# Early denominators in a tile of their own, low words converted on GpSimd, and a new order table, in an attention and feed-forward kernel with a built-in planner

## The chip, the core and the metric

The kernel runs on one core of one Trainium2 chip. The metric is the device time of one execution in microseconds; lower is better. Below, PE is the matrix engine, DVE the vector engine, ACT the scalar engine, POOL the GpSimd engine, and SP the queue from which this kernel issues all its DMAs.

## The reference

Linear attention with exponential features over 8 batches, 8 heads, 576 tokens and head size 64, then a feed-forward layer over 4608 tokens:

```python
def phi(x):
    proj = einsum('bhsd,df->bhsf', x, w_phi)                 # d = 64, f = 128
    proj = proj - max(abs(proj), axis=-1, keepdims=True)
    return concatenate([exp(proj), exp(-proj)], axis=-1)
q_p, k_p = phi(q), phi(k)
kv  = einsum('bhsf,bhsd->bhfd', k_p, v)
z   = sum(k_p, axis=2)
num = einsum('bhsf,bhfd->bhsd', q_p, kv)
den = einsum('bhsf,bhf->bhs', q_p, z)[..., None] + 1e-06
x   = (num / den) as [4608 tokens, 512]
h   = x @ w_in                                               # 512 x 2048
out = maximum(h, 0) ** 2 @ w_out                             # 2048 x 512
```

The two weight matrices arrive as 64-bit words, each of a high and a low 32-bit half.

## The kernel before

**Pairs.** Attention is done for 32 pairs of heads, p = 0 to 31; four pairs make a batch. The first six pairs are done by `early(p)`, the others by `visit` and `late`. For an early pair the steps are: project the keys (L604, L610), take the greatest absolute value of each row and subtract it on DVE (L620, L623, L630, L633), exponentials on ACT (L626 to L638), key-value product on PE (L660, L665, L693), eviction and transposition (`kvs`, `kz`, L705); the same for the queries (L721, L727, L732, L734, L755, L764, L766); numerators (L774, evicted into `n`), denominators (L791). The denominators of pair p are copied from PSUM by `copy` (L310) into the scratch tile `sx`, from there a DMA (L799) takes four rows of `sx` into `den`, DVE adds and inverts (L808, L809), a DMA writes `rd` (L812) and two more spread it into `rb` (L819). DVE multiplies `rb` by `n` (L826); ACT and DVE split the product into two 16-bit parts and write them into the token ring (L845, L848).

**Scratch.** `sx` has one buffer and two kinds of user: the early denominators, and `batch_scale`, whose ACT scans (L567) write their elementwise result there only to have somewhere to write it; what counts is their accumulator, the greatest absolute value of each pair's `v`. `batch_scale` of the first batch needs the scans of v_0 to v_3; its result goes through a DVE reduction (L572, tile `m`), a transposition on PE (L397) and a few short DVE operations.

**Weights.** There are 16 pieces of 1024 KB, 8 of `w_in` (raw0i to raw7i) and 8 of `w_out` (raw0o to raw7o). `join_words` turns the word pairs of a piece into one float, tile `u`. It scales the high half (`size`, ACT L451), converts the low half to three bits (`low`: ACT L460, DVE or POOL L462, by the piece's number in `order_w`), and joins them. Pieces of even number write the low half as 16-bit values into the lower half of the high word (`low_half`) and need `shift` (L465) and `join` (L472); those of odd number write 32-bit values (`low_word`) and need `ends` (L468) and `join_shift` (L476). `w_in` then needs its greatest value (`most`, ACT L498), a scale (`power`, PE L397, DVE L403 to L408) and two parts (`value_in`, ACT L547, DVE L550); `w_out` three parts (L517; L306 on POOL or DVE; L535 on ACT or L537 on DVE).

**Feed-forward.** Tokens go in 18 chunks of 256, the hidden dimension in 8 steps: the first product (L1027, 24 matmuls into `ph`), three ACT operations (L1036, L1038, L1040), one on DVE (`gl`, L306), and the second product (L1057, 12 matmuls into `po`). The first chunk needs the ring entries of pairs 0 to 3, and step f needs piece f of both matrices.

**The order.** Every operation is given to a planner (`Plan`) with an engine, a time in us, what it follows and which tiles it uses; some have a second engine (`other`). `order` simulates the engines with these times and takes at each step the ready operation of the lowest rank; the instructions are then written engine by engine in that order, and each engine works through its list in order. The ranks of the early operations come from the table `RANKS`, two characters for each. Tiles with one buffer and several kinds of user (`single`) are free again at `open_at`. Where `lock` is given, the planner lets DVE and POOL operations delay each other.

Of the kernel before, what the change touches and what calls it, by code (L numbers as in the profile page):

```python
# [292 lines left out]
def tile_kernel(ctx, tc, qp, kp, vp, w_phi, w_in, w_out, out):  # L293
# [269 lines left out]
    def batch_scale(b, rank):  # L563
        last = []
        for i in range(NP):
            p = b * NP + i
            last.append(P.add("ACT", 0.78, lambda p=p, i=i: A.activation(  # L567
# [103 lines left out]
    def early(p):  # L671
# [127 lines left out]
        o = P.add("SP", 0.65, lambda: SP.dma_start(  # L799
            den_[p], sx_["d", p][0:128:32, 0:SH].rearrange("j (r x) -> j r x", x=9)), [o], use + [("den", p)],  # L800
# [354 lines left out]
    "IfI<I3=WN$W(Y>a6S2MOP)TpPYLwQJ@TBuI#N%NGIFF;HZLSMHA5>EICS3O?LrRGJJF_@$G]Q-P,JELKGI=OD(P3GXUyO`NnR{K`"
    "NuV#MsLmL0WO[lV-N>E>=IT8Q^WIE*O$MZIYDuO.H5Lx?:I(FiMdE0K=LVM*T5M<J+HoAsHZQ?LeS_M>S>LjI9WCQjAQEa:(:o<J"
    "=ZC!=$;HC)?+Co7(6(?l?B5N<k@>?=@u9@9l73?-F.BMBm>?JwH^LMLY@JMh>*+y:L3qF[?UCX<`5K?hG_]0B-AyB7@ZC^EXE[CV"
    "N_DXRHKlI6QL@J@QDNPrFxNoO0NjHeL(N_RWZ0FEE9KTH,G$R;D(H4>EC<5h:JBhE_CiHUIGJIC%FT:2B!=RDKP?8XA|F)BTMl;Z"
    "?RHe:89c@wA<>*;<=L?oAX<?7dAo3J>[D21M?<7I46;T<&:/B!FWK_KKJ_O0LdEu>*1s;TE,BJGeOfR8U}PnJtVuLIYgB/FuG0B."
    "Dq7wF#@V?2==319hGfM.JLLzPMY17zB[A[A.@4@ZF7HaVQRBMaK7R}Cu?<HxB4FaBX@Q6rCk;IC+D-:*/DKcJHGpOGE*T0QaDOPO"  # L1160
    "RNEC_U^gP]AOETIxATILM6G5=rQ^C0<tB<OaJeTjT7LMY*L>L{IiK?Ht@S>.R*QYO]PZLkIn:4Jd9wBY>dSeJSWlN>G}CsPRKp<z"
    ";]>nIK^SD-F^6oAhGfR1MSVKD.4W?0AqB|8t77HOAj@OL-CY@{A-KXB8PfN[Q{L0NBM(KqHBMxKi?r<V7n19<+BFDFMyC(P|XFZ/"
    "LXI)L%:&D%Ke?XT{M8U>BvR9LeE.E=</?D;u>=B25D=_9e0i:K,u5g4@0T&o1h#22G9`8I:,7x8+Av>Z0*20*{$&(V.[9Z>5J_UJ"
# [47 lines left out]
```

## Time and profile before

| | |
|---|---|
| median of 3 runs | 1077.39 us (1074.45 to 1078.67) |
| span of the profiled execution, first to last instruction | 1074.6 us |
| mean granted clock of PE | 0.984 |
| PE busy | 1032.4 us, 96% of the span |
| DVE busy | 742.0 us, 69% |
| ACT busy | 632.7 us, 59% |
| POOL busy | 140.5 us, 13% |
| first matmul of the first product (L1027) | 112.46 us |

For the profiled execution the page gives the span alone. It is 2.8 us under the median of the runs and lies at the lower end of what they spread over. Shares are averages over the whole span; a table of stretches of time is needed to see where an engine waits.

### The profile page before, as it was taken

How to read it: one execution, taken by the hardware profiler on the slowest of the kernel's cores; microseconds unless marked ns; L12 is line 12 of the kernel's file. 1: busy time of each engine (PE TensorE's matmuls, PEld its weight loads, DVE VectorE, ACT ScalarE, POOL GpSimd, SP SyncE). 2: the span in 40 equal slices, each digit the busy share in tenths (PEclk: the TensorE clock that was granted, in tenths of full speed). 3: DMA queues.
4: the chain of work that ended last, by engine and by line, in shares of the span. 5: the costliest groups of instructions: out<-in, count | busy, mean ns of one | idle time of the engine just before them, and what ended most of it. 6: DMA issues, size and time to landing. Idle time of an engine off the chain costs nothing.

```text
span 1074.6 us, 19448 instructions
## 1 busy us (share of the span) xinstructions
PE 1032.4 (96%) x7675; PEld 708.0 (66%) x7762; DVE 742.0 (69%) x1550; ACT 632.7 (59%) x1125; POOL 140.5 (13%) x70
## 2 busy tenths in 40 slices
...
GB/s 361 185 131 114 131 127 44 67 76 56 65 61 80 58 50 72 56 76 57 76 46 74 53 58 45 64 56 76 43 53 28 48 11 42 12 21 20 1 21 20
DMA packets 66143, 73.47 MB, mean 68 GB/s; under 512 B 35204, under 2 KB 44036, under 8 KB 64004
## 3 DMA queue, kind: packets, MB, share of 16 engines
q1 hardware_dynamic: 66052, 72.22, 21.3%
q8 instruction: 61, 1.00, 0.4%
...
## 4 chain that ended last, share of the span: by engine, by line
PE 83%; DVE 1%; issue 1%; ACT 0%
PE po L1057 34%; PE ph L1027 33%; PE pv L660 4%; PE pn L878 3%; PE pp L604 2%; PE pv L878 2%; PE pp L948 2%; PE pn L948 1%; PE pv L665 1%; PE pn L610 1%; DVE wl L537 0%; DVE gl L306 0%; PE pn L397 0%; DVE den L808 0%; ACT sx L567 0%
## 5 line engine op out<-in xcount | busy, mean ns | idle before, releaser
L1027 PE MATMUL ph<-ring,win 128*128 128x256 f16 x3456 | 399.7, 273 | 0.2 <-DVE gl L306 0.2
L1027 PEld LDWEIGHTS <-win 128*128 128x128 f16 x3456 | 336.2, 98 | 69.8 <-issue 8.7
L1036 ACT ACTIVATE r<-ph,cw 128x512 f32<-128x512 f32 x144 | 98.9, 687 | 241.0 <-PE ph L1027 240.7
L306 DVE TENSOR_TENSOR gl<-ph,gh 128x512 bf16<-128x512 f32 x144 | 98.3, 682 | 174.7 <-ACT ph L1040 171.6
L961 POOL PARTITION_ALL_REDUCE mx<-pt x52 | 113.2, 2176 | 618.6 <-ACT pt L310 363.0
L1057 PE MATMUL po<-wh,gh 128*128 128x512 f32 x576 | 171.6, 419 | 0.0
L1057 PE MATMUL po<-wl,gl 128*128 128x512 bf16 x560 | 147.1, 379 | 0.9
L1057 PE MATMUL po<-wl,gh 128*128 128x512 bf16 x505 | 134.6, 381 | 4.7
L1057 PEld LDWEIGHTS po<-wh,gh 128*128 128x128 f32 x576 | 98.5, 189 | 29.2 <-issue 10.9
L1057 PEld LDWEIGHTS <-gl 128*128 128x128 bf16 x576 | 56.4, 98 | 68.0
L1038 ACT ACTIVATE gh<-r 128x512 fp32r<-128x512 f32 x144 | 90.6, 629 | 4.8 <-PE po L1057 0.5
L1057 PEld LDWEIGHTS <-gh 128*128 128x128 bf16 x576 | 44.8, 98 | 73.3 <-issue 39.7
L1040 ACT ACTIVATE ph<-r 128x512 f32<-128x512 f32 x144 | 84.1, 584 | 0.3
L660 PE MATMUL pv<-e,v 128*64 128x256 f32 x512 | 62.6, 385 | 0.8 <-ACT n L310 0.6
L975 DVE SCALAR_TENSOR_TENSOR pt<-qe,zc,pt 128x576 f32<-128x576 f32 x52 | 42.3, 815 | 26.0 <-ACT pt L973 25.4
L310 ACT ACTIVATE n<-pn 128x320 f32<-128x320 f32 (+1 forms) x32 | 13.7, 429 | 70.9 <-PE pn L878 69.3
L626 ACT ACTIVATE e<-e 128x512 f32<-128x512 f32 x64 | 39.7, 621 | 23.8 <-DVE e L623 23.7
L306 DVE TENSOR_TENSOR qe<-pt,mx 128x576 f32<-128x576 f32 x52 | 39.1, 752 | 16.7 <-POOL mx L961 16.3
L660 PEld LDWEIGHTS pv<-e,v 128*64 128x64 f32 x512 | 36.2, 139 | 17.3 <-issue 1.8
L966 ACT ACTIVATE qe<-qe 128x576 f32<-128x576 f32 x52 | 35.0, 672 | 19.8 <-DVE qe L306 19.8
L912 DVE STREAM_TRANSPOSE kvs<-pv 128x256 f32<-128x256 f32 x26 | 11.6, 447 | 48.6 <-PE pv L878 46.0
L973 ACT ACTIVATE pt<-qe,zc 128x576 f32<-128x576 f32 x52 | 40.1, 773 | 4.2
...
## 6 DMA issues: line engine op xcount, KB each, us to landing
v<-in_vp_dram SPq DMA_DIRECT2D x32, 320.0 KB
k<-in_kp_dram SPq DMA_DIRECT2D x32, 288.0 KB
q<-in_qp_dram SPq DMA_DIRECT2D x32, 288.0 KB
...
raw0i<-in_w_in_dram SPq DMA_DIRECT2D x1, 1024.0 KB
```

What stands on the lines that cost most here:

```text
L306: eng.tensor_tensor(out=out_, in0=a, in1=b_, op=ALU.subtract)
L626: o = P.add("ACT", act_us(512), lambda n=n: A.activation(out=e_[n][:, :, 1, :], in_=e_[n][:, :, 0, :], func=AF.Exp, scale=-1.0), [o], [("e ...
L660: PE.matmul(out=to[64 * h:64 * h + 64, 0:256], lhsT=v_[p][:, t, h, :], rhs=e_[2 * p + h][:, t].rearrange("p s f -> p (s f)"), start=t == 0 ...
L878: PE.matmul(out=to[64 * h:64 * h + 64, :], lhsT=kz_[n][:, 128 * s_ + 64 * h:128 * s_ + 64 * h + 64], rhs=qe_[2 * n + h].rearrange("p (s x) ...
L961: o = P.add("POOL", par_us(S), lambda n=n, h=h: G.partition_all_reduce(mx_[n], pt_[p][:, h, :], channels=128, reduce_op=bass_isa.ReduceOp. ...
L973: o = P.add("ACT", act_us(S, 1), lambda h=h, qe=qe, y=y: A.activation(out=y(), in_=qe(0), func=AF.Copy, scale=zc_[p][:, 2 * h:2 * h + 1]), ...
L975: o = P.add("DVE", dve_us(S), lambda h=h, qe=qe, y=y: V.scalar_tensor_tensor(out=y(), in0=qe(1), scalar=zc_[p][:, 2 * h + 1:2 * h + 2], in ...
L1027: PE.matmul(out=ph[:, j, :], lhsT=win[w][:, t, 128 * ff:128 * ff + 128], rhs=ring[half][x][:, t, c0:c0 + T], start=k == 0, stop=k == 3 * K ...
L1036: o = P.add("ACT", act_us(512, 1), lambda: A.activation(out=r_[n], in_=ph_[bank], func=AF.Relu, scale=cw[:, f, 0:1]), [g1], [("ph", bank), ...
L1038: sq = P.add("ACT", act_us(512), lambda: A.activation(out=gh_[n], in_=r_[n], func=AF.Square), [o], [("r", n), ("gh", n)], Q)
L1040: o = P.add("ACT", 0.59, lambda: A.activation(out=ph_[bank], in_=r_[n], func=AF.Square), [o], [("ph", bank), ("r", n)], Q, other=("DVE", 0 ...
L1057: PE.matmul(out=po_[po[i][1]], lhsT=g[:, j, 128 * i:128 * i + 128], rhs=w[:, j, :], start=(ff == 0 and s == 0), stop=(ff == 2 * NFP - 1 an ...
```

## The change

The early denominators are evicted into a tile `dn` of their own (one buffer, 128 x 288) in place of `sx`, and the DMA into `den` reads that tile. All 16 low halves are converted on POOL as 16-bit values, and all pieces use `shift` and `join`; L460, L468 and L476 are no longer issued. In the planner a single tile counts as free when the DMA that reads it has landed (`op.there`), not when it is issued (`op.end`), and four costs are altered. The table `RANKS` is another one throughout.

```diff
-                open_at[tag] = max(open_at.get(tag, 0.0), op.end + self.HOP[op.eng])
+                open_at[tag] = max(open_at.get(tag, 0.0), op.there + self.HOP[op.eng])
...
+    dn_ = tiles(at, "dn", [128, SH], F32, 1)
...
         def low(E):
-            to = (low_half if n % 2 == 0 else low_word)()
+            to = low_half()
...
-        x = (("ACT", 1.15, A, None), ("DVE", 0.68, V, 4.0), ("DVE", 0.68, V, 4.0), ("POOL", 2.4, G, 0.0))[n % 4]
-        l = P.add(x[0], x[1], lambda: low(x[2]), [sz], [], rank, lock=x[3])
-        if n % 2 == 0:
+        l = P.add("POOL", 1.15, lambda: low(G), [sz], [], rank, lock=0.0)
+        if True:
             o = P.add("DVE", 0.68, shift, [sz], key, rank, lock=4.0)
             o = home_read[home] = P.add("DVE", 1.22, join, [o, l], key, rank, lock=4.0)
...
-        most_in[f] = ... P.add("ACT", 1.06, most, [o], [("u", n)], rank)
+        most_in[f] = ... P.add("ACT", 1.2, most, [o], [("u", n)], rank)
...
-                P.add("DVE", 0.69, lambda: near(V), at, key, rank, lock=0.6, other=("ACT", 1.06, lambda: near(A), None))]
+                P.add("DVE", 0.69, lambda: near(V), at, key, rank, lock=4.0, other=("ACT", 1.06, lambda: near(A), None))]
...
-            last.append(P.add("ACT", 0.78, lambda p=p, i=i: A.activation(     # the scans of v
+            last.append(P.add("ACT", 0.82, lambda p=p, i=i: A.activation(
...
-        use = [("sx", ("d", p))]
+        use = [("dn", p)]
...
-        first, second = copy(SH, lambda: sx_["d", p][:, 0:SH], lambda: pn_["d", p][:, 0:SH])
+        first, second = copy(SH, lambda: dn_[p], lambda: pn_["d", p][:, 0:SH])
...
-            den_[p], sx_["d", p][0:128:32, 0:SH].rearrange("j (r x) -> j r x", x=9)), [o], use + [("den", p)],
+            den_[p], dn_[p][0:128:32, :].rearrange("j (r x) -> j r x", x=9)), [o], use + [("den", p)],
...
-            o = P.add("DVE", dve_us(S), lambda h=h, qe=qe, y=y: V.scalar_tensor_tensor(
+            o = P.add("DVE", 0.82, lambda h=h, qe=qe, y=y: V.scalar_tensor_tensor(
...
-    ">e8[J.LRL]EQRBCsO#Ij?@IlF+FbHa@4DoEsJ%^S^INpLYIVR=PXNlY^ADJUQ^J`CNEmD{HgLQLSIeL(UZL[L(F^KXLxC#DLBV<5"
+    "<qBAE1E)s^H&zzcLa5V*AUf&DrX2o]yH.gH[I?MG/a0+M+CD1*hmN<O+4TsLOCZpL)JrM7KOm#c1VeP|9MRTO^W4L9I9SKv@a$F*"
```

What the table moves is read from the order in which the instructions stand. The number at a row's start is its place on its engine; numbers after a name are those of the buffer. Lines below L351 carry a number one higher after the change (L465 becomes L466), up to where both agree again in `split_in`.

The first place is ACT around the scans of v (L567, which write `sx` and the accumulator `vm`). Before, the scan of v_3 stands behind the eviction of denominators 0 into the same scratch:

```order
26 L451 ACTIVATE u_1_341<-raw1i_142 128x1024
27 L567 ACTIVATE sx_2_352,vm_0_157<-v_2_144 128x640
28 L310 ACTIVATE sx_3_363<-pn_4_343 128x288
29 L764 ACTIVATE qe_2_371<-pp_2_356 128x2x288
30 L766 ACTIVATE qe_2_371<-pp_2_356 128x2x288
31 L567 ACTIVATE sx_4_400,vm_0_157<-v_3_163 128x640
32 L498 ACTIVATE raw1i_142,wm_0_93<-u_1_341 128x1024
```

The same engine after the change:

```order
15 L567 ACTIVATE sx_2_263,vm_0_143<-v_2_126 128x640
16 L567 ACTIVATE sx_3_266,vm_0_143<-v_3_138 128x640
17 L310 ACTIVATE kvs_0_281<-pv_0_218 128x384
18 L567 ACTIVATE sx_4_284,vm_1_285<-v_4_140 128x640
19 L498 ACTIVATE raw0i_124,wm_0_93<-u_0_216 128x1024
20 L626 ACTIVATE e_3_287<-e_3_287 128x4x128
21 L628 ACTIVATE e_3_287<-e_3_287 128x4x128
22 L452 ACTIVATE u_1_319<-raw1i_147 128x1024
```

The four scans of the first batch now stand in rows 2, 3, 15 and 16, ahead of the second weight piece; denominators 0 go to `dn_0` in row 36 and denominators 1 to the same buffer in row 52. On SP, the loads of v_2 and v_3 stood in rows 13 and 15 behind five weight pieces, and stand in rows 9 and 10 behind one.

The second place is POOL at the start (L306 is the low part of `w_out`, L462 or L463 the conversion of low halves). Before:

```order
8 masks.py:199 AFFINE_SELECT ident_72<-ident_72 128x128
9 L462 TENSOR_SCALAR raw2i_140<-raw2i_140 128x1024
10 L306 TENSOR_TENSOR wl0_691<-u_4_581,wh0_676 128x1024
11 L306 TENSOR_TENSOR wl0_691<-u_2_513,wh0_676 128x1024
12 L306 TENSOR_TENSOR wl1_938<-u_6_869,wh1_921 128x1024
13 L462 TENSOR_SCALAR raw4i_126<-raw4i_126 128x1024
14 L306 TENSOR_TENSOR wl1_938<-u_8_1003,wh1_921 128x1024
```

After:

```order
11 L463 TENSOR_SCALAR raw0o_308<-raw0o_308 128x1024
12 L463 TENSOR_SCALAR raw2i_185<-raw2i_185 128x1024
13 L463 TENSOR_SCALAR raw1o_166<-raw1o_166 128x1024
14 L463 TENSOR_SCALAR raw3i_145<-raw3i_145 128x1024
15 L306 TENSOR_TENSOR wl0_642<-u_2_523,wh0_621 128x1024
16 L826 TENSOR_TENSOR rb_0_598<-n_0_384,rb_0_598 128x576
17 L463 TENSOR_SCALAR raw2o_719<-raw2o_719 128x1024
18 L306 TENSOR_TENSOR wl0_642<-u_4_560,wh0_621 128x1024
19 L463 TENSOR_SCALAR raw4i_170<-raw4i_170 128x1024
20 L463 TENSOR_SCALAR raw3o_154<-raw3o_154 128x1024
21 L463 TENSOR_SCALAR raw5i_180<-raw5i_180 128x1024
```

Rows 9 and 10 there are the conversions of raw0i and raw1i. POOL does ten conversions, two low parts and one product with `rb` up to row 21; before it did two conversions and four low parts up to row 14.

The third place is DVE at the ring entry of pair 3 (the last L848 row), the last one that the first chunk needs. Before:

```order
126 L468 SCALAR_TENSOR_TENSOR raw4i_126<-raw4i_126 128x1024
127 L476 SCALAR_TENSOR_TENSOR u_7_999<-u_7_999,raw4i_126 128x1024
128 L472 SCALAR_TENSOR_TENSOR u_8_1003<-raw3o_184,u_8_1003 128x1024
129 L732 TENSOR_REDUCE qm_5_1056<-pp_11_1031 128x4
130 L462 TENSOR_SCALAR raw5i_177<-raw5i_177 128x1024
131 L734 TENSOR_TENSOR pt_5_1062<-pp_11_1031,qm_5_1056 128x512
132 L732 TENSOR_REDUCE qm_5_1056<-pp_11_1031 128x4
133 L537 CAST wl1_938<-u_8_1003 128x1024
134 L734 TENSOR_TENSOR pt_5_1062<-pp_11_1031,qm_5_1056 128x512
135 L826 TENSOR_TENSOR rb_3_1052<-n_3_956,rb_3_1052 128x576
136 L468 SCALAR_TENSOR_TENSOR raw5i_177<-raw5i_177 128x1024
137 L848 SCALAR_TENSOR_TENSOR ring0_1_79<-rb_3_1052,cb_82,ring0_0_78 128x576
```

After:

```order
117 L473 SCALAR_TENSOR_TENSOR u_7_926<-raw4i_170,u_7_926 128x1024
118 L826 TENSOR_TENSOR rb_2_960<-n_2_871,rb_2_960 128x576
119 L466 TENSOR_SCALAR u_8_939<-u_8_939 128x1024
120 L473 SCALAR_TENSOR_TENSOR u_8_939<-raw3o_154,u_8_939 128x1024
121 L466 TENSOR_SCALAR u_9_965<-u_9_965 128x1024
122 L848 SCALAR_TENSOR_TENSOR ring0_1_79<-rb_2_960,cb_82,ring0_0_78 128x576
123 L473 SCALAR_TENSOR_TENSOR u_9_965<-raw5i_180,u_9_965 128x1024
124 L466 TENSOR_SCALAR u_6_769<-u_6_769 128x1024
125 L826 TENSOR_TENSOR rb_3_1006<-n_3_1021,rb_3_1006 128x576
126 L473 SCALAR_TENSOR_TENSOR u_6_769<-raw2o_719,u_6_769 128x1024
127 L732 TENSOR_REDUCE qm_5_1069<-pp_11_1047 128x4
128 L848 SCALAR_TENSOR_TENSOR ring0_1_79<-rb_3_1006,cb_82,ring0_0_78 128x576
```

The ring entry of pair 3 moves from row 137 to row 128 on DVE. Counted by line from the fifth row on to that entry: L462 three times 32-bit and twice 16-bit before, none after; L468 and L476 nine times before, none after; L465 and L472 ten times before, twenty after; L537 three times before, none after; L826 four before, three after; L732 and L734 of 512 columns 24 before, 21 after; `win` on DVE (L547's second engine) and one eviction none before, one each after. All else is equal. On PE the first L1027 matmul stands in row 324 in both orders, with the same work ahead of it but for a few short pieces; from row 3,500 of 10,424 on PE does the same in the same order but for some 140 rows between 6,500 and 7,100.

More of the change, by code (lines that the diff above doesn't have):

```diff
@@ L498, in most @@
             A.activation(out=spare[f]().bitcast(F32), in_=u_[0][n].bitcast(F32), func=AF.Abs, accum_out=wmax[g][:, i:i + 1])
-        most_in[f] = home_read[home_of[f, True]] = P.add("ACT", 1.06, most, [o], [("u", n)], rank)
+        most_in[f] = home_read[home_of[f, True]] = P.add("ACT", 1.2, most, [o], [("u", n)], rank)
         return o
@@ L1153 @@
 RANKS = (
-    ">e8[J.LRL]EQRBCsO#Ij?@IlF+FbHa@4DoEsJ%^S^INpLYIVR=PXNlY^ADJUQ^J`CNEmD{HgLQLSIeL(UZL[L(F^KXLxC#DLBV<5"
[L1155 to L1163, printed above, removed]
@@ L1164 @@
-    "G+Y%CA>;8(=x>&Gy:3I#HsIR;1?pLu@$IOH5K)JPECAWZzCyY^XnG:V:QtP1F<GK6KGpL,D6=WE,L!VWg2h3Q^SJU.h.g@PgK?Ob"
-    "Yb]f]f^0^<X8SIT:ijo{],bSaVhQYtey_ScAXASJUjM@WecHPTJe`2VhSVUViaXPLtW5VALLE2=sKVL<TDLTLzPGLO[F`Na}Z=XR"
-    "P,N&J5VTE|N^18>1ApQ]IXAC7D3v-=(d/U*v7b.Y8Q4;/HG6D)E!G=LeLAS=N[YG]rGPRlA&W%MMXqYhV>PgTORCFdPhC&Gt<xB^"
-    "DYFnL<EtGGJI@bJ/FIO@TV_CUHZpUiIlRB<&G0M,0[2H0]JP9(?j>Z@<D{D>Db?IK$<8>*BtJS0oM6ArM(Du8TL/C5A?UBU@P?L]"
-    "9Z<k=OA%MaG2IgC-HIG.MJJ+D9NoQO^ye(SDR9Y-KlJnUDjgW1C9H|8BH9C:DNEd4^?LE#AX<X?@NwQwM7J8>#@}>7AgD&Fs?NKD"
@@ L1174 @@
-    "O2Lp=+KTF<HZ92>SH:<RHaIPS_Z!S*YfN*JGJHJ7HdI*`^J@HrPDNKQc?_FWHO?>JfFBD=>+KLOoS;W$KU;1RdPSNRMNWnhrnkbX"
-    "_?T&V3eEUfR[Ji>qPtJCN$S4J[^FVwLq_}FOE_QrUScj]x_,e>kX_#Q-WxUC^ueyas^RQ@__[vP`Y#X8NGF;Wk`zS]I=Ko``_aIr"
-    "a^cnWhY]TJb;`&"
+    "<qBAE1E)s^H&zzcLa5V*AUf&DrX2o]yH.gH[I?MG/a0+M+CD1*hmN<O+4TsLOCZpL)JrM7KOm#c1VeP|9MRTO^W4L9I9SKv@a$F*"
+    "^LCvGEfF4^h^SrKqUz=ScNA3YI`zQ-1WY-y$M^AWC$OgN>9QV2KGR1DIKDS@7TX|=PAO.-5]Rv]IIsq0]:]&CLAZ/M.-J7Ih6@:P"
+    "F3j9.M7G<P4EpjP;Xy:vMP3OJn>=>?AaRRd}E>F0l8SOL/z%8EFD8GJnGIbjNt>5ko18BI[J]*Rw7b9(0SA_B<e_8tExC7VQ;PAE"
@@ new lines @@
+    "LlZJ>{Y?Os8Y<iBh@VLBI3Bt8OJF@nb./6K+KVPuJYj:Xn]TQ];?DlOEP|FoZpS}V%grKj?s`!M5MVPr>}X_>TbbL?IQBZ.GKf@="
+    "/.>xL;CX`Ilc?!>R9.2XY0<[Iiikl91o:x>6E*.-cS57:rm83@0A<;;}B8UKPL?6YzKQK+S0K!W2B=p#O]Wm<0;XNrL,JtROW9X."
+    "VtKa[`K^/1Y|5:16UO.-9+HD>M4@?]>a:w4QI^<N6rPO60cL@8[i./ueMzOD?hSNDkgy.wN-.7FQ=]InL+]#VVMau%]:05UWJPc*"
+    "VDL};FP2PD1bH}]DMw?{<)ZbXPO1DLPDT0pBs}m!<X[]Z?U?[4Be50=WJVG3Pm/`I&CKOjR_7zAePwC==60RAh:c;%FcPo;cGmMV"
+    "FK[j]hTTvsN(X1Cqa1T*2PLx8)Yz.-Ez<I`(I)f8>o_8l}]&D9C+L=Pw6jLR=]Wp0cL&A{F%mQB{_h.4@xGI9n52H`DDL8O;T6_F"
@@ new lines @@
+    "<oImXc;nVwDL0GMQ_07m9xD+QTqw?*.;F3Nne$Fc^X:$.RJ80lF*PV?o7{>DANXF^30<FXu[<BQFG7DhHkYCoNG9I{`>c&.-KO/o"
+    ">-TX/fFqMFJ<jyO5WF6gdkR2NNKpII=t^*E!YhSe@,dKLPI4V,4i9Xa1BJUtWiC_@I@i5(K)]-9QJ>Ao/fY}MGQL=|{ApY0XPfy4"
+    "BR97@,69NHEB@uWxHJE)[_1OR!7f1Zb<SxOcKaP_]POPT_NNRf1uN&G0D&UXOnNT3QT,M!BaNoB#=!ZU3+V/]@JoU:6*oQH&fjn_"
+    "R):!L%an^<Zp0bi98(@C5JK@WDMTHa9:Vjvy_.o$JmK1Ok@ni:]DshU&/5UPT2Y{CxM@NX3aW:QW:CEbWhnC=9PG3nV2dO]PKPp9"
+    "KsW;c|BHHIC}K,GnJ*_j=mVFHKLiU?UpZK0>I{lN.5H}TD0-i/y4:*55O.lZXKTHWxHD<.K)IhGgWAZ/Q#LK7ga%mmX71mE0D*B5"
@@ new lines @@
+    "o$Rld_3kj7F>`u[?J>K$P<e*pDU4>FF{0d`WA!BLZB4L5KgBA}zW]4Wmf2<^[`HH<%C_RdmyES.-Kw9k;g8NgJ3y0r;q.ZJQeWYF"
+    "Num-H}2cS3J,==Gn=<W-]:?qPWzZABe`;r>K:pUr4Q1+W-I[Ce8SUz3l4b9c0-8wOhER>x9Q9v2}6iV/V{HM<eUKeo:ddChLCFHa"
+    "BxAvWBc^4oXI8$I|>6O|NUSc<E176GM5O:G}`Zv>[ASuDD/>dJHm;`?S]^yKJ-KxayW_@5XKg2=3a?LlF20bR/15=n:x=d4hAEKU"
+    "9.@.;!b@MJ.-ah>K]WbeDvg2inIDQiJ!<6WpcVGUUsMhPaW!]d5_.N^JEe?G0PqwS|O-1PK0N-V>bzC%<p]J3[R/T5H{:G9SvGRV"
+    "93.HJ*^hslWwE1978d3(G1:8Nr7J{$?95uFk5nMJjp3uFK<?R%0.Rx]uZ_XAKCI<bhXkbeIhCXKy64VrQ:F+f0CIZaOQ9PALGk.-"
```

10 lines of the change are left out of this document (5 added, 5 removed).

## The prediction

> **What bounds the kernel now.** I read the table of stretches first, then PE's waits in the timeline up to the first matmul of the first product (L1027), then the groups of DVE, ACT and POOL up to that moment. The stretches, with the busy time of each engine:
>
> ```profile
> core 0: us, PE busy (x) PEld busy (x) DVE busy (x) ACT busy (x) POOL busy (x), PEclk, DMA share, GB/s
> 5.00:112.40 107.40, 80.83 (x835) 51.66 (x832) 80.08 (x134) 81.29 (x138) 12.94 (x7) 0.84 0.55 199
> 45.00:112.40 67.40, 51.83 (x564) 32.63 (x562) 61.06 (x95) 58.08 (x95) 11.54 (x5) 0.86 0.38 116
> 112.40:165.00 52.60, 50.83 (x389) 34.38 (x387) 49.96 (x79) 40.53 (x64) 9.47 (x5) 1.00 0.36 116
> 165.00:350.00 185.00, 183.99 (x1357) 127.20 (x1370) 153.47 (x334) 120.23 (x224) 37.27 (x17) 1.00 0.22 65
> 350.00:1075.00 725.00, 716.33 (x5106) 494.25 (x5172) 458.14 (x1000) 389.34 (x700) 80.47 (x37) 1.00 0.16 46
> ```
>
> From 112.4 us on PE is the bound: it idles 1.8 us of 52.6, then 1.0 of 185 and 8.7 of 725, at a granted clock of 1.00. Its work there cannot shrink, since both programs have the same matmuls. Ahead of 112.4 it idles 26.6 of 107.4 us at a mean clock of 0.84, and that is the only time to be had. From 45 us on DVE is busy 91% of the time and ACT 86%; PE waits for both, and the first L1027 starts right behind the last ring entry on DVE:
>
> ```profile
> 39.42 0.77 PE L397 MATMUL pn<-ident,m 128*128 128x128 f32 x2 [7.20 <-DVE m L572]
> 97.34 0.66 PE L755 MATMUL pp<-ident,pt 128*128 128x128 f32 x4 [3.74 <-DVE e L623]
> 102.15 2.08 PE L721 MATMUL pp<-wraw,q 64*128 64x128 f32 x16 [3.86 <-ACT qe L766]
> 111.51 0.81 DVE L848 SCALAR_TENSOR_TENSOR ring<-rb,cb,ring 128x576 f16<-128x576 f32 x1
> 112.46 2.79 PE L1027 MATMUL ph<-ring,win 128*128 128x256 f16 x24
> ```
>
> So the end moves with the moment of that ring entry, as long as PE stays full afterwards. I work the sum at this point.
>
> **Part 1, the tile of its own.** The longest wait ahead of it:
>
> ```profile
> 29.16 0.70 SPq L799 DMA_DIRECT2D den<-sx  x1
> 38.25 0.74 ACT L567 ACTIVATE sx<-v 128x640 bf16<-128x640 f32 x1 [7.63 <-DMA den<-sx]
> DVE m L572 <- ACT sx L567: 8.7, 1, 8.7
> ```
>
> The scan of v_3 writes the scratch that the DMA of denominators 0 still reads; the DMA takes 9.1 us from issue to the scan's start. DVE then idles 8.7 us, PE 7.2. With `dn` this wait has no cause. What is late next: the scans of v_2 and v_3 now wait for their loads only. Summing the loads ahead of them in SP's order with these sizes
>
> ```profile
> v<-in_vp_dram SPq DMA_DIRECT2D x32, 320.0 KB
> k<-in_kp_dram SPq DMA_DIRECT2D x32, 288.0 KB
> raw0i<-in_w_in_dram SPq DMA_DIRECT2D x1, 1024.0 KB
> 21.32 1.12 POOL L462 TENSOR_SCALAR raw2i<-raw2i 128x1024 int32<-128x1024 uint32 x1 [11.69 <-DMA raw2i<-in_w_in_dram]
> ```
>
> (q has the size of k, the first load 192 KB), v_3 is complete after 3,648 KB, where it was after 8,768. In before raw2i was complete at 6,080 KB and landed at 21.3 us, so v_3 is there well ahead. raw1i is now complete at 6,016 KB, so ACT reaches it at about 21 us with little or no wait. The `dn` buffer itself is read until at most 9 us after its first DMA; fifteen ACT rows, exponentials, scans and scalings, stand between its two writers, some 11 us at the scan's 0.74. I take the whole 8.7 us; the bounds are 0 (another wait in its place) and 8.7.
>
> **Part 2, the low words, and what the new order moves past the ring entry.** The rows of DVE and ACT up to 112.4 us:
>
> ```profile
> L462 DVE TENSOR_SCALAR raw1i<-raw1i 128x1024 int32<-128x1024 uint32 x1 | 0.7, 685 | 0.0
> L462 DVE TENSOR_SCALAR raw0o<-raw0o 128x1024 uint16<-128x1024 uint32 x1 | 1.3, 1322 | 0.0
> L468 DVE SCALAR_TENSOR_TENSOR raw1i<-raw1i 128x1024 int32<-128x1024 int32 x1 | 1.2, 1226 | 0.0
> L465 DVE TENSOR_SCALAR u<-u 128x1024 int32<-128x1024 int32 x5 | 3.4, 697 | 1.2 <-ACT u L451 1.2
> L472 DVE SCALAR_TENSOR_TENSOR u<-raw1o,u 128x1024 int32<-128x1024 int32 x1 | 1.2, 1226 | 0.0
> L537 DVE CAST wl<-u 128x1024 bf16<-128x1024 f32 x3 | 6.7, 2239 | 0.0
> L826 DVE TENSOR_TENSOR rb<-n,rb 128x576 f32<-128x576 f32 x4 | 3.0, 749 | 0.0
> L734 DVE TENSOR_TENSOR pt<-ph,qm 128x512 f32<-128x512 f32 x10 | 6.6, 687 | 4.0 <-PE pp L759 3.9
> L460 ACT ACTIVATE raw0i<-raw0i 128x1024 uint16<-128x1024 uint32 x1 | 2.5, 2549 | 0.0
> L517 ACT ACTIVATE wh<-u 128x1024 fp32r<-128x1024 f32 x4 | 4.2, 1060 | 0.6 <-DVE u L472 0.6
> 164.31 0.69 DVE L537 CAST wl<-u 128x1024 bf16<-128x1024 f32 x1
> ```
>
> By the counts of rows ahead of the ring entry of pair 3, DVE loses three conversions of 0.69 and two of 1.32 (4.7 us); nine joins of 1.23 (11.0) against five shifts of 0.70 and five joins of 1.23 (9.6), so 1.4; three casts, at the undisturbed 0.69 of the last row (2.1); one product moved to POOL (0.75); three subtractions or maxima of 0.69 (2.1); and gains one scaling at the 0.69 of a conversion and one eviction of at most 0.69 (1.4). That is 9.7 us less DVE work ahead of the entry. ACT loses three conversions of 2.5 (7.5), and by its own list two L517 of 1.06; its other differences, one piece more or less each of about 1.1, cancel. So ACT is relieved by some 9.7 us too, beside the wait of part 1, and does not become the bound. None of it stands under cover: DVE is the engine that the entry waits for, at 91% busy.
>
> **Part 3, POOL's price.** POOL now has ten conversions ahead of the entry, and DVE suffers from what POOL does:
>
> ```profile
> 90.97 1.45 POOL L462 TENSOR_SCALAR raw4i<-raw4i 128x1024 int32<-128x1024 uint32 x1
> 106.27 2.36 POOL L306 TENSOR_TENSOR wl<-u,wh 128x1024 bf16<-128x1024 f32 x1 [13.85 <-ACT wh L517]
> 106.68 2.50 DVE L537 CAST wl<-u 128x1024 bf16<-128x1024 f32 x1
> 123.24 2.01 POOL L462 TENSOR_SCALAR raw6i<-raw6i 128x1024 int32<-128x1024 uint32 x1
> 151.46 1.17 POOL L462 TENSOR_SCALAR raw7o<-raw7o 128x1024 int32<-128x1024 uint32 x1 [15.72 <-DMA raw7o<-in_w_out_dram]
> ```
>
> The cast that starts under POOL's 2.36 us operation takes 2.50 in place of 0.69. The Trainium skill (SBUF — State Buffer, Who interferes with whom) says that a DVE instruction in a two-port mode, or with two inputs in SBUF, and a GpSimd instruction exclude each other for the whole of the one that came first. By that rule the trace's 2.50 is 1.95 us of waiting and 0.69 of work, and it agrees; the rule speaks against the change, and what it would make of all ten conversions is the slower rival below.
>
> In before the three casts together lost 3 x (2.24 - 0.69) = 4.7 us under 11.5 us of POOL work after 45 us, 0.40 us for each us of POOL. No row shows a 16-bit conversion on POOL. Bounds: 1.12, the fastest 32-bit row, and 2.46, if it grows as ACT's did against an equal 32-bit pass (2.55 against the 1.16 of its row in the timeline).
>
> ```profile
> 12.38 1.16 ACT L451 ACTIVATE u<-raw0i 128x1024 f32<-128x1024 f32 x1 [0.19 <-DMA raw0i<-in_w_in_dram]
> ```
>
> I take the mean of POOL's four rows, 1.44, since engine and input are the same there. Ten of them, two low parts of 2.36 and a product of at most 1.4 (2.36 x 576/1024) make 20.5 us of POOL ahead of the entry; at 0.40 that costs DVE 8.2 us, 3.5 more than the 4.7 of before. The bounds: nothing blocked (4.7 less than before) and every conversion of 2.46 blocking DVE for its whole length (24.6 + 6.1 - 4.7 = 26 more). POOL itself is far from full, 20.5 us of some 95.
>
> **Part 4, planner and table.** The counting until landing only changes the order: no DMA reads a single tile any more, and the altered costs change no instruction. Behind the first L1027 the order differs up to row 3,500 of PE; there PE idled 1.8 us in 52.6 and DVE was 95% busy. DVE has less to do there too (the remaining conversions and double joins), so I take no change, with bounds of 1.8 us less and some 3 more, one stall like those at 97 us.
>
> **The sum.** -8.7 - 9.7 + 3.5 = -14.9 us at the ring entry, so the first L1027 at about 97.6. Work on PE ahead of it fits: 80.8 us busy at a clock of 0.84 in 92 us, with fewer gaps. Span 1074.6 - 14.9 = 1059.7. The median of the runs is 2.8 us above this span, so 1062.5 in its terms.
>
> **The rivals.** *Half the gain (0.17).* One of the two large terms is taken by another wait: without part 1, -6.2 gives 1071; without part 2, because DVE's 27 us of idle time ahead of 112.4 grow instead, -5.2 gives 1072. For it: beside the 8.7, DVE idles 18.6 us there on chains of several engines, which less work does not shorten. Against: from 45 us on 91% is full, and the 3.9 us behind PE's L759 in the L734 row above are two waits that PE itself would end sooner.
>
> *More than forecast (0.10).* The lock costs nothing since the planner now spaces near casts away from POOL: -8.7 - 9.7 - 4.7 = -23.1, so 1054. For it: no cast on DVE stands ahead of the entry any more. Against: joins have two inputs in SBUF and there are ten.
>
> *Slower: POOL blocks DVE (0.08).* Conversions of 2.46 us exclude DVE for their whole length; +26 - 18.4 = +7.6, so 1085. It decides from about 1.8 us per conversion, all blocked: the 18.4 us gained and 4.7 less the 6.1 of POOL's other work, over ten. For it: both other engines took about twice as long for 16-bit results, and the cast above was blocked whole. Against: DVE's operations on PSUM, half of its rows there, ran beside POOL at their usual 0.68.
>
> *No change (0.08).* The shorter start is given back behind it: weight pieces 6 and 7 arrive when they did, and PE waits where it had work, or the conversions cost near the decisive length. 1073 to 1082. Against: the last piece's join has some 19 us less DVE work ahead of it than before, counted the same way.
>
> **How the numbers follow.** The forecast has 0.57 and covers 1056 to 1069, by the two prices of a conversion at 0.40 (10 x 1.02 x 0.40 = 4.1 up, 1.3 down) and part 4. With the gains of the half case up to 1074 and most of the better one from 1054, the range holds about 0.82. Within 0.5% of 1077.4 (5.4 us, about what this measurement can tell from no change) is 1072.0 to 1082.8. Of the half case 0.06 falls there: faster 0.78, same 0.14, slower 0.08.
>
> **What would show it.** Right: no ACT scan waits for the denominators' DMA; L462's successor on POOL between 1.1 and 1.5 us; no L460, L468, L476; first L1027 at 94 to 101; PE's idle time from there to 165 us no more than 2 to 3. Wrong: POOL conversions near 2.5 with joins stretched beyond 2 us, PE idle behind the first L1027, or a new wait of ACT for raw1i at 21 us with the exponentials queued behind it.

## The result, and the profile after

| | before | after |
|---|---|---|
| median of the runs | 1077.39 us (1074.45 to 1078.82) | 1072.18 us (1070.57 to 1072.93) |
| span of the profiled execution | 1074.6 us | 1068.8 us |
| ring entry of pair 3 starts (L848) | 111.51 us | 95.76 us |
| first L1027 matmul | 112.46 us | 100.33 us |

The ratio is 0.995, 95% interval 0.9933 to 0.9966: a gain of 5.2 us where 14.9 were forecast. The ring entry moved by 15.8 us, the first product by 12.1, the end by 5.8 (spans of the two profiled executions). The stretches of the kernel after, cut at the end of that entry, and then at its first L1027 (columns as before):

```profile
core 0: us, PE busy (x) PEld busy (x) DVE busy (x) ACT busy (x) POOL busy (x), PEclk, DMA share, GB/s
5.00:96.57 91.57, 76.30 (x779) 49.30 (x781) 82.99 (x125) 71.90 (x133) 35.61 (x15) 0.85 0.64 236
...
5.00:100.30 95.30, 80.03 (x837) 51.68 (x837) 86.69 (x127) 73.60 (x135) 39.34 (x16) 0.86 0.63 231
100.30:165.00 64.70, 57.81 (x426) 41.06 (x427) 59.57 (x97) 42.11 (x68) 30.36 (x12) 0.97 0.25 82
165.00:350.00 185.00, 184.13 (x1367) 125.75 (x1378) 147.70 (x323) 116.52 (x216) 31.62 (x14) 1.00 0.23 67
```

Up to the entry DVE's idle time fell from 27.3 us to 8.6, but with 9 instructions fewer DVE is busy 2.9 us longer (82.99 against 80.08). Behind the start PE idles 6.9 us of 64.7, where it idled 1.8 of 52.6. POOL works 35.6 us up to the entry; it worked 12.9. The rows of DVE and POOL there, from the timeline and from the groups of DVE's instructions, and behind them L808 and L848 in the kernel before:

```profile
13.52 2.55 POOL L463 TENSOR_SCALAR raw0i<-raw0i 128x1024 uint16<-128x1024 uint32 x1 [2.68 <-ACT u L452]
14.28 2.33 DVE L466 TENSOR_SCALAR u<-u 128x1024 int32<-128x1024 int32 x1
73.57 2.35 DVE L808 TENSOR_SCALAR den<-den 128x9 f32<-128x9 f32 x1
83.24 2.50 POOL L463 TENSOR_SCALAR raw5i<-raw5i 128x1024 uint16<-128x1024 uint32 x1
83.36 3.18 DVE L473 SCALAR_TENSOR_TENSOR u<-raw4i,u 128x1024 int32<-128x1024 int32 x1
95.76 0.81 DVE L848 SCALAR_TENSOR_TENSOR ring<-rb,cb,ring 128x576 f16<-128x576 f32 x1
L466 DVE TENSOR_SCALAR u<-u 128x1024 int32<-128x1024 int32 x10 | 13.6, 1358 | 0.0
L808 DVE TENSOR_SCALAR den<-den 128x9 f32<-128x9 f32 x4 | 5.5, 1368 | 0.0
L848 DVE SCALAR_TENSOR_TENSOR ring<-rb,cb,ring 128x576 f16<-128x576 f32 x4 | 4.5, 1113 | 0.0
L473 DVE SCALAR_TENSOR_TENSOR u<-raw2i,u 128x1024 int32<-128x1024 int32 x1 | 3.2, 3172 | 0.0
L473 DVE SCALAR_TENSOR_TENSOR u<-raw0o,u 128x1024 int32<-128x1024 int32 x1 | 2.0, 1957 | 0.0
```

```profile
L808 DVE TENSOR_SCALAR den<-den 128x9 f32<-128x9 f32 x4 | 1.4, 344 | 0.0
L848 DVE SCALAR_TENSOR_TENSOR ring<-rb,cb,ring 128x576 f16<-128x576 f32 x4 | 3.2, 810 | 0.6 <-ACT ring L845 0.6
```

A conversion takes 2.5 us or more (2.48 to 3.09), not 1.44. The shifts, joins, ring entries and L808 that start on DVE under one end only after it, while DVE's operations on PSUM run beside it at their usual 0.68. The shift at 14.28 starts 0.76 us into the conversion and takes 2.33 us in place of 0.70. The ten shifts lose 6.6 us together, three of the ten joins (3.18, 3.17 and 1.96 for 1.23) 4.6, the four L808 on nine numbers per partition 4.1, the four ring entries 1.3: some 17 us of DVE's time, where the forecast had 8.2.

The wait of part 1 is gone: no scan waits for the denominators. What PE waits for now ahead of its stalls, and the chain behind the stall at 125 us:

```profile
83.09 0.95 PE L755 MATMUL pp<-ident,pt 128*128 128x128 f32 x6 [2.42 <-DVE e L623]
88.38 1.12 PE L755 MATMUL pp<-ident,pt 128*128 128x128 f32 x4 [2.23 <-ACT qe L766]
112.00 2.48 POOL L463 TENSOR_SCALAR raw5o<-raw5o 128x1024 uint16<-128x1024 uint32 x1 [1.29 <-issue]
112.57 2.46 DVE L466 TENSOR_SCALAR u<-u 128x1024 int32<-128x1024 int32 x1
115.14 2.22 DVE L473 SCALAR_TENSOR_TENSOR u<-raw6i,u 128x1024 int32<-128x1024 int32 x1
117.40 1.17 ACT L498 ACTIVATE raw6i<-u 128x1024 f32<-128x1024 f32 x1 [5.44 <-DVE u L473]
122.31 0.67 ACT L1036 ACTIVATE r<-ph,cw 128x512 f32<-128x512 f32 x1
121.53 5.12 POOL L306 TENSOR_TENSOR wl<-u,wh 128x1024 bf16<-128x1024 f32 x2 [5.25 <-ACT wh L517]
121.67 2.76 DVE L537 CAST wl<-u 128x1024 bf16<-128x1024 f32 x1
124.35 0.68 DVE L306 TENSOR_TENSOR gl<-ph,gh 128x512 bf16<-128x512 f32 x1
125.08 4.25 PE L1027 MATMUL ph<-ring,win 128*128 128x256 f16 x24 [3.93 <-DVE gl L306]
```

Read it from below. PE waits 3.93 us for `gl`. On DVE `gl` stands behind a cast that POOL's low part stretched to 2.76 us. Its input comes from ACT, whose first operation for that step starts only at 122.31: ACT had stood 5.44 us for the join of raw6i, which stood behind a shift of 2.46 us under the conversion of raw5o, and then another 1.76 us for the join of raw4o.

### The profile page after: what moved, and what is told of

Read it like the earlier page. It is cut to its first block, busy times and chain, and to the rows that moved or that the text cites. A ratio compares the mean times of both kernels' runs of the same rounds, so it can differ in the third digit from the quotient of the medians.

```text
span 1068.8 us, 19448 instructions
## 1 busy us (share of the span) xinstructions
PE 1032.6 (97%) x7673; PEld 708.1 (66%) x7762; DVE 749.2 (70%) x1544; ACT 621.7 (58%) x1117; POOL 184.9 (17%) x84
## 4 chain that ended last, share of the span: by engine, by line
PE 84%; DVE 1%; issue 1%; ACT 0%
PE po L1057 34%; PE ph L1027 34%; PE pv L660 4%; PE pn L878 3%; PE pp L604 2%; PE pv L878 2%; PE pp L948 2%; PE pn L948 1%; PE pv L665 1%; PE pn L610 1%; DVE e L623 0%; DVE u L473 0%; DVE km L620 0%; PE pv L774 0%; PE pn L398 0%
## 5 line engine op out<-in xcount | busy, mean ns | idle before, releaser
L1027 PE MATMUL ph<-ring,win 128*128 128x256 f16 x3456 | 400.7, 273 | 3.9 <-DVE gl L306 3.9
L1027 PEld LDWEIGHTS <-win 128*128 128x128 f16 x3456 | 337.1, 98 | 73.7 <-issue 11.5
L306 DVE TENSOR_TENSOR gl<-ph,gh 128x512 bf16<-128x512 f32 x144 | 98.6, 685 | 174.4 <-ACT ph L1040 172.9
L306 DVE TENSOR_TENSOR qe<-pt,mx 128x576 f32<-128x576 f32 x52 | 39.2, 753 | 24.4 <-POOL mx L961 24.1
```

The costliest lines, as they stand in the source:

```text
L306: eng.tensor_tensor(out=out_, in0=a, in1=b_, op=ALU.subtract)
L1027: PE.matmul(out=ph[:, j, :], lhsT=win[w][:, t, 128 * ff:128 * ff + 128], rhs=ring[half][x][:, t, c0:c0 + T], start=k == 0, stop=k == 3 * K ...
```

## The experiments

In all of them the figure behind "measured" is the median, and the ratio to the kernel before with its 95% interval. The changed kernel stands at 0.995.

**Price alone.** On a spare tile from 913 us on, POOL, ACT and DVE one after the other each do six conversions of 128 x 512 numbers: 32-bit integers or floats into every second 32-bit word (as `low_word`), into every fourth 16-bit half (as `low_half`), and into adjoining ones.

```diff
+  E.tensor_scalar(out=to(), in0=of(), scalar1=0.875, scalar2=0.4995, op0=ALU.mult, op1=ALU.add)   # POOL, DVE
+  A.activation(out=to(), in_=of(), func=AF.Copy, scale=0.875, bias=0.4995)                        # ACT
```

> The changed kernel with eighteen extra operations on a spare tile behind the last ring entry, where DVE and POOL have little else to do: 128 x 512 elements on POOL, ACT and DVE, each as 32-bit words to 32-bit words with a step of two words, to 16-bit values with a step of four, to 16-bit values side by side, to 32-bit words side by side, float to float, and float to bfloat16 with a step of four. If the 16-bit result alone makes a conversion long: POOL 1.2 to 1.3 us in both 16-bit integer forms and 0.6 in the 32-bit ones, ACT alike. If it is the scattered writing: only the forms with a step of four are long, bfloat16 too. If it is the integer type: bfloat16 is short. The time of the whole kernel stays at 1072.

Groups by form; the last numbers are the busy time and the mean of one in ns:

```profile
L1153 POOL TENSOR_SCALAR px<-px 128x512 int32<-128x512 uint32 x2 | 1.3, 639 | 20.0 <-DVE px L1156 20.0
L1153 POOL TENSOR_SCALAR px<-px 128x512 uint16<-128x512 uint32 x2 | 2.0, 986 | 0.2
L1153 POOL TENSOR_SCALAR px<-px 128x512 f32<-128x512 f32 x1 | 0.7, 657 | 0.1
L1153 POOL TENSOR_SCALAR px<-px 128x512 bf16<-128x512 f32 x1 | 1.3, 1332 | 0.1
L1151 ACT ACTIVATE px<-px 128x512 uint16<-128x512 uint32 x2 | 2.0, 988 | 0.1
L1153 DVE TENSOR_SCALAR px<-px 128x512 uint16<-128x512 uint32 x2 | 1.2, 590 | 0.1
```

Each uint16 group holds one scattered and one adjoining case. On POOL the slowest of all its forms took 1.352 us and the fastest 0.619, and two of mean 0.986 are just these: 1.35 scattered and 0.62 adjoining. The float forms show the same, 1.33 for scattered 16-bit results against 0.66 for 32-bit ones in the same tile. So it is neither the integer type nor the 16 bits alone but 16-bit results written 8 bytes apart that cost twice as much on POOL. ACT (1.35 at most) does the same; on DVE it is 0.75 at most against 0.42 for 32-bit words, a factor of 1.8. This single run took 1068.7 us where 1072 was expected.

**Parts of the change with the table unchanged.** Three kernels took one part each and kept the table they came with:

```diff
e1: before, with  use = [("dn", p)] and the tile dn
e2: after, with   to = (low_half if n % 2 == 0 else low_word)() and the engines of before
e3: after, with   to = low_word(), ends and join_shift for all pieces, low words on POOL
```

> The kernel before with one thing changed: early denominators are evicted into a tile of their own. Theory A (the prediction's part 1): ACT's wait of 7.6 us for the denominators' DMA goes, DVE's 8.7 us idle with it, and nothing else takes its place: 1067 to 1070, ratio 0.991 to 0.993, first L1027 at 104 to 106. Rival B (another wait takes its place, so what the whole change gained came from its table): 1074 to 1077, ratio above 0.997.

> The changed kernel with its new tile and its new table, but the low words converted as before: four on ACT as 16-bit values, eight on DVE, four on POOL as 32-bit values. Theory A (POOL's 16-bit conversions of 2.5 us exclude DVE and took back the gain): DVE's work grows by about 12 us, but the blocking of 17 us ahead of the ring entry falls to about 6, so it ends no slower than the changed kernel, 1066 to 1072, and the 3.9 us wait of PE behind the first product is gone. Rival B (the new table itself leaves PE without work behind the first product): that wait stays, 1073 to 1080.

> The changed kernel with all sixteen conversions on POOL, but as 32-bit words, joined with two DVE operations of 1.22 us in place of 0.69 and 1.23. Theory A: a conversion takes 1.1 to 1.4 us in place of 2.5, so POOL is shorter by some 18 us and DVE is blocked for less; against that DVE works 16 x 0.53 = 8.5 us more. 1066 to 1071. Rival B (what POOL does matters little, DVE's own work sets the start): slower than the changed kernel by a good part of the 8.5 us, 1074 to 1079.

Measured: 1088.41 (1.0103, 1.0086 to 1.0119), 1103.15 (1.0248, 1.0226 to 1.0269), 1104.71 (1.026, 1.0244 to 1.0276). All missed every expectation. The ranks of the table hold for one list of operations; with other tiles or engines the planner puts other operations first, and PE, DVE and ACT run in another order. In the first, the first product starts at 96.52, 16 us earlier than before, and PE then runs dry (stretches, and a row of ACT):

```profile
125.00:150.00 25.00, 17.29 (x122) 10.14 (x121) 20.35 (x45) 16.64 (x27) 1.60 (x2) 0.86 0.19 50
150.00:200.00 50.00, 38.82 (x239) 25.91 (x238) 34.58 (x56) 28.21 (x42) 13.91 (x7) 0.90 0.23 80
158.35 1.15 ACT L452 ACTIVATE u<-raw7i 128x1024 f32<-128x1024 f32 x1 [5.52 <-DMA raw7i<-in_w_in_dram]
```

They tell nothing on the parts, but two things on the method: an early first L1027 is not an early end, and a part has to be tried with the order held.

**The tile of its own, order held.** Before's order row for row; the planner still reckons with `sx`.

```diff
+    dn = at.tile([128, SH], F32, name="dn")
-        first, second = copy(SH, lambda: sx_["d", p][:, 0:SH], ...
+        first, second = copy(SH, lambda: dn, ...
```

> The kernel before with its own order kept row for row on every engine; only the eviction of the early denominators and the DMA behind it use a tile of their own in place of sx. Theory A (the wait of the scan of v_3 for that DMA is worth what it lasts, 8.7 us): first L1027 near 104, median 1068 to 1070. Theory B (other waits of the same chain take its place, since the rows of ACT and DVE around it stand where they stood): the wait goes and another of 3 us or more appears, first L1027 at 108 or later, median 1072 to 1077.

Measured: 1067.09 (0.9906, 0.9891 to 0.992), theory A. The scan of v_3 now stands right behind the exponentials. The start moves by 9.4 us, and nearly all of it reaches the end (spans 1074.6 and 1065.5). First two rows of the timeline, then the stretch up to the start:

```profile
28.46 0.74 ACT L567 ACTIVATE sx<-v 128x640 bf16<-128x640 f32 x1
103.10 2.79 PE L1027 MATMUL ph<-ring,win 128*128 128x256 f16 x24
```

```profile
5.00:103.10 98.10, 77.97 (x835) 50.19 (x834) 81.34 (x134) 80.34 (x138) 12.86 (x7) 0.90 0.61 218
```

Against the kernel before PE idles 6.4 us less in this stretch (20.1 for 26.6); the other 2.9 us are the same matmuls at a granted clock of 0.90 in place of 0.84.

**The price, order held.** The changed kernel's order on every engine; only the size or form of POOL's conversions differs.

```diff
f2, f4: to, of = to[:, 0:m], low_w()[:, 0:m]...     # m = 512, m = 128
f3:     to = low_word()                              # 32-bit, not taken up by the join
```

> The changed kernel, same order on every engine; POOL converts only 512 of each piece's 1024 low words (the other half is left out), so a conversion should take about 1.3 us in place of 2.5. Theory A (the price of the conversions on POOL, and what they block on DVE, is where the forecast gain went): DVE's stretched shifts and joins shorten with them, first L1027 near 95 and PE idle less between it and 165 us, median 1058 to 1065. Theory B (the gain is lost on chains that POOL has no part in): median 1069 to 1073.

> The changed kernel, same order; POOL writes its results as 32-bit words into the low word in place of 16-bit values into the high word, and the join does not take them up (the low bits are left out). A conversion takes 1.1 to 2.0 us, the price that the prediction used (1.44). Theory A: median 1058 to 1066, first L1027 at 94 to 98. Theory B: 1069 to 1073. If A holds here but the median stays above 1063, part 1 or 2 of the sum was too large as well.

> The changed kernel, same order; POOL converts 128 of each piece's 1024 low words (the rest is left out), about 0.4 us each. With the half-sized conversions it gives the slope. Theory A: each us of POOL time taken away ahead of 125 us is worth 0.3 to 0.6 us of the whole, so 12 conversions of 2.1 us less give 8 to 15 us: median 1057 to 1064. Theory B: 1068 to 1073.

Measured: half 1059.21 (0.9837, 0.982 to 0.9853), words 1059.93 (0.9842, 0.9826 to 0.9858), an eighth 1056.11 (0.9808, 0.9793 to 0.9822). Theory A in the first two; the eighth comes out 0.9 us below its range. With half the conversions (1.34 to 1.92 us each) the same order and the same DVE instructions give, up to the first L1027 at 93.78:

```profile
5.00:93.80 88.80, 75.82 (x836) 49.31 (x835) 74.84 (x128) 73.90 (x135) 25.80 (x16) 0.94 0.69 249
93.80:165.00 71.20, 67.44 (x506) 47.18 (x509) 64.19 (x118) 50.19 (x82) 28.08 (x14) 1.00 0.26 86
L466 DVE TENSOR_SCALAR u<-u 128x1024 int32<-128x1024 int32 x10 | 8.4, 839 | 1.1 <-ACT u L452 1.1
```

13.5 us less on POOL, 11.9 less on DVE (shifts 8.4 for 13.6). PE's idle time behind the start is 3.8 us in place of 6.9. Between the changed kernel and this one the price is worth 1.1% of the time before (0.995 less 0.9837), some 12 us.

**On which side of the start.** The ten conversions ahead of pair 3's ring entry halved, or the six behind it.

```diff
+            m = 512 if n < 10 else 1024     # g2: n >= 10
+            to, of = to[:, 0:m], low_w()[:, 0:m]...
```

> The changed kernel, same order; only the ten conversions that stand ahead of the ring entry of pair 3 are halved (512 of 1024 low words, the other half left out), the six behind it stay whole. Theory A (the price acts on both sides of the first L1027): first L1027 near 94 as with all sixteen halved, but a stall of 2 to 4 us stays behind it, median 1062 to 1066, two thirds of the 13.0 us that all sixteen gave. Theory C (what stands behind the entry is covered, as the prediction had it): 1058 to 1061.

> The changed kernel, same order; only the six conversions behind the ring entry of pair 3 are halved (the other half of their low words left out). Theory A: first L1027 stays at 100, the 3.9 us of PE idle at 125 shrinks, median 1067 to 1070. Theory C: no change, 1071 to 1073.

Measured: 1063.93 (0.9876, 0.9861 to 0.9891) and 1064.27 (0.9882, 0.9866 to 0.9898). First the timeline of the one, then of the other:

```profile
90.67 5.41 PE L1027 MATMUL ph<-ring,win 128*128 128x256 f16 x48
115.58 4.37 PE L1027 MATMUL ph<-ring,win 128*128 128x256 f16 x24 [3.93 <-DVE gl L306]
```

```profile
100.63 5.42 PE L1027 MATMUL ph<-ring,win 128*128 128x256 f16 x48
123.09 2.78 PE L1027 MATMUL ph<-ring,win 128*128 128x256 f16 x24 [1.89 <-DVE gl L306]
```

Conversions ahead set the start, those behind it the stall. The first is theory A, though its start comes 3 us sooner than expected. The second has theory A's signs (the start stays, the stall shrinks), but it gains more than both ranges allow: 1064.27 where A had 1067 to 1070 and C 1071 to 1073. Each alone gives more than half of what both give (0.74 and 0.68 of 1.13%); why they overlap is open. The starts also show what a single trace is worth: with the same ten conversions halved, L1027 starts at 90.67 here and at 93.78 above.

**Scratch shared again, new order held.**

```diff
-    dn_ = tiles(at, "dn", [128, SH], F32, 1)
+    sd = at.tile([128, 320], F32, name="sd")     # for the scans and the denominators
```

> The changed kernel, same order, but denominators and scans share one scratch tile again. Theory A (the tile of its own is worth its wait in this order too): some scan or eviction waits for the DMA into den again, 3 to 9 us, median 1075 to 1082. Theory D (the new order alone, with the scans of the first batch ahead of denominators 0, already avoids the wait): 1071 to 1074.

Measured: 1073.6 (0.9967, 0.9955 to 0.998), theory D: 1.4 us above the changed kernel, and the two intervals overlap. The wait is there again, but smaller (in all, times, longest; it was 7.6 us in one):

```profile
ACT sd L567 <- DMA den<-sd: 3.3, 2, 2.2
```

The new table alone, with the scans of the first batch ahead of denominators 0, removes more than half of the wait that the tile removes in the old order, and most of what it cost.

**Other engines and forms for the whole computation, order held.** Each at the places that POOL's conversions, the shifts and the joins have:

```diff
h1: low(G) into low_word; nothing at the shift's place, ends() and join_shift() at the join's
h2: low(G if of_in else A) into low_half
h3: as h1 with low(A)
h4: as h1 with low(G if of_in else A)
```

> The changed kernel, same order; all low words are converted on POOL into 32-bit words at 1.1 to 2.0 us and are all used: shift and join give way to ends and join_shift, both at the join's place (DVE 2.45 us per piece in place of 1.93). Theory A (only POOL's price and its blocking of DVE ate the gain): 1.2 us less on POOL for each conversion against 0.5 more on DVE, median 1063 to 1068. Rival B (DVE's own work decides as much as POOL's price): 1070 to 1075.

> The changed kernel, same order, but the eight conversions of w_out are issued on ACT (16-bit, 2.55 us) at the place that POOL's had; w_in stays on POOL. Theory A: DVE is freed of half of the blocking, and ACT takes 13 us more ahead of the ring entry, 73.6 plus 13 of 95: median 1065 to 1069. Rival B (ACT becomes the engine that PE waits for): 1073 to 1080.

> The changed kernel, same order; all low words are converted on ACT into 32-bit words (about 1.15 us, 16 times), ends and join_shift on DVE at the join's place. POOL blocks no shift or join any more. Theory A: DVE loses the 17 us of blocking ahead of the entry and gains 5 of work, ACT gains 12: median 1061 to 1066. Rival B (ACT becomes the bound): 1070 to 1076.

> As the one with all words on ACT, but w_in's low words on POOL and only w_out's on ACT. Theory A: between the two whole ones, 1062 to 1066. Rival B: 1070 or more.

Measured: h1 1066.3 (0.9909, 0.9894 to 0.9923), h2 1071.6 (0.9957, 0.9942 to 0.9973), h3 1071.86 (0.9959, 0.9944 to 0.9975), h4 1066.93 (0.9919, 0.9906 to 0.9933). Words on POOL give theory A. With ACT in POOL's place (h2, h3) nothing is gained against the changed kernel: h3 is rival B, and h2 lies between its two ranges. ACT is late for PE in h3,

```profile
91.20 1.11 PE L755 MATMUL pp<-ident,pt 128*128 128x128 f32 x4 [3.90 <-ACT qe L766]
```

in an order that had no room for it. h4 lies 0.9 us above theory A's range and below rival B's.

**The price and an order searched for it.** Three kernels whose planner reckons the measured prices, each with a table of ranks found by a search on the planner's own simulation:

```diff
i1: after, l = P.add("POOL", 2.55, low(G)...)
i2: after, low words into low_word, ACT 1.15 (other: DVE 0.69), ends and join_shift
i3: before with dn, prices 2.55 (ACT), 0.69, 1.32 (DVE), 1.6 (POOL)
```

> The changed kernel whose planner reckons 2.55 us for a conversion on POOL (1.15 before), with a table of ranks searched for that price. Theory A (the price itself is the loss; an order that knows it can only hide a part): median 1068 to 1072. Rival E (the loss came from an order searched at the wrong price; with the right one the change gives what was forecast): 1060 to 1064.

> The changed kernel with all low words converted into 32-bit words on ACT (1.15 us) or DVE (0.69), ends and join_shift on DVE, nothing of it on POOL, and a table of ranks searched for these prices. Theory A (without the 16-bit price and without the blocking the gain of the first two terms is kept): median 1060 to 1066, below every kernel that computes the whole so far. Rival B (ACT's and DVE's own work decides): 1068 to 1073.

> The kernel before with the tile of its own for denominators and its mixture of engines for the low words, whose planner reckons their measured prices (2.55 on ACT, 1.32 on DVE for 16 bits, 1.6 on POOL for words), and a table of ranks searched for them. Theory A: 1062 to 1067, at or a little below the 1067.1 of that kernel in its own order. Rival E (a new table is worth more than any price): below 1060.

Measured: i1 1066.73 (0.9903, 0.9889 to 0.9918), i2 1058.96 (0.9838, 0.9825 to 0.9852), i3 1061.77 (0.9862, 0.9846 to 0.9878). i1 lies below theory A's range and above rival E's: about half a per cent was lost with an order that took a conversion for 1.15 us. i2 and i3, which do without 16-bit conversions on POOL, come out another 5 to 8 us lower (i2 1.0 and i3 0.2 us below theory A's range). That points to the price, but each of them has a table of its own as well. i2 beats both kernels, and in it PE starts L1027 at 94.15; in i1 it starts later than after (106.58 against 100.33), and i1 ends earlier, since behind its start PE idles only 0.1 us up to 165 us:

```profile
94.15 5.40 PE L1027 MATMUL ph<-ring,win 128*128 128x256 f16 x48
```

```profile
106.58 5.41 PE L1027 MATMUL ph<-ring,win 128*128 128x256 f16 x48
```

## Why the prediction was wrong

**Part 3 is the term that was mis-sized.** It put a conversion at 1.44 us "since engine and input are the same there", although it had the doubling of ACT's rows in hand and 2.46 as its upper bound. The output decides: 16-bit results 8 bytes apart cost twice as much (the price alone), and the value chosen came from rows with another output. Measured: 2.48 to 3.09 us each, POOL 35.6 us up to the entry in place of 20.5 (its two low parts and the product took 8.4 us in place of 6.1), DVE's loss some 17 us in place of 8.2. The share of POOL's time that DVE loses was near, 17 of 35.6 or 0.48 against 0.40. The sign written down for wrong, conversions near 2.5 with joins stretched beyond 2 us, is what the trace shows. One sign written down for right held all the same: the first L1027 at 100.33 lies within 94 to 101.

**The step that failed is "the end moves with the moment of that ring entry", with part 4's "I take no change" behind the first L1027.** At the entry the sum came out, 15.8 us earlier against 14.9, but by luck, since two errors cancel: DVE lost 9 us more to POOL, and its idle time shrank by 18.7 us, not by the 8.7 of the one wait. L1027 did not follow the entry. Before, it started 0.95 us after the entry started. In the new order it starts 4.3 to 4.6 us after it in all eleven traces of that order, also with conversions of an eighth (89.87 and 94.20). There the maximum right ahead of the entry on DVE (L732) reads what L721 on PE has just written, and some 5 us of other PE work stand between L721 and L1027. In the kernel after DVE even waits for PE; the first row belongs to the chain told next:

```profile
86.58 1.15 ACT L498 ACTIVATE raw4i<-u 128x1024 f32<-128x1024 f32 x1 [1.47 <-DVE u L473]
95.15 0.69 DVE L732 TENSOR_REDUCE qm<-pp 128x4 f32<-128x512 f32 x1 [0.86 <-PE pp L721]
```

So PE set the start, and not DVE. What made PE late is the wait at 88 us. The conversion of raw5i (83.24) stretches the join of raw4i to 3.18 us, ACT waits 1.47 us for that join, and `qe` (L766), for which PE waits until 88.38, stands behind that wait on ACT. From there PE works for 11.95 us without a gap, up to 94 us at half clock (last section).

Of the entry's 15.8 us 3.6 were lost between the entry and L1027, by the order and not by the price. Another 6.3 were lost behind the start. Up to 165 us PE idles 5.1 us more there than before (6.9 for 1.8), 3.9 of it in the stall at 125 us, and its clock is 0.97 in place of 1.00; the upper bound of "some 3 more, one stall" was too small. The two halved kernels show that the conversions act on both sides. The first L1027 is no measure of the end either: it stands at 96.5 in the kernel of 1088.4 and at 106.6 in that of 1066.7.

With a price near the assumed one the same order gives 1059.2 (halved, 1.53 us in the mean) and 1059.9 (words), 3 us under the forecast 1062.5: price and blocking make the whole of the miss and a little more. The path is still not the forecast's: with half the conversions the entry starts at 89.45, 22.1 us earlier than before, and 3.4 of these are lost between it and L1027.

**Part 1 was right in mechanism and near in size.** 8.7 us were forecast, 9.4 measured with the old order, of which 6.4 are PE's waiting and the rest a higher clock that the term did not have. Not foreseen: in the new order the tile is worth only some 1.4 us, which lies within the spread, since the scans stand ahead of the denominators there. The scans, `m` (its PE row at 39.42 before, at 20.47 after) and raw1i behaved as written.

**Part 2** can't be timed apart from an order. What DVE's rows say: 82.99 us busy less some 17 lost to POOL is 66, against 80.08 less the 4.7 of before, or 75.4, so 9.4 us less work, as the term of 9.7 had it. ACT fell by 9.4 us too (81.29 to 71.90, the latter up to the entry), against 9.7.

**The rivals.** The price of "POOL blocks DVE" came true, but not its condition: DVE lost about half of POOL's time, not all, because its operations on PSUM ran beside POOL, as the rival's "against" had it. The end did not go above before. The "no change" rival named the place, the stretch behind the start; the price was well above its decisive length of 1.8 us (its sum gives 1.7), which held for full blocking only. It had 0.08 and came within 1 us. The half gain's 1071 to 1072 is the time that came out, by none of its reasons.
